# RWKV attention and GELU MLP on one core: orders behind the first MLP products searched at build, half of the negative powers made on ScalarE, the decays' transfer issued by ScalarE

## The chip, the cores and the metric

The kernel runs on one core of a Trainium2 chip. The metric is the device time of one execution in microseconds (us), as the median of several runs. Engines are named as in the profile: PE (TensorE matmul), PEld (TensorE weight load), DVE (VectorE), ACT (ScalarE), POOL (GpSimd) and SP (SyncE, which issues most transfers).

## The reference

A linear attention with decay per head and channel runs over 768 positions for 4 batches and 8 heads of 48 channels, and its output, 3072 tokens of 384 channels, goes through an MLP with 2048 hidden units.

```
for t in range(S):                       # S = 768, D = 48, f32
    cur = einsum('bhd,bhe->bhde', u * k[:, :, t], v[:, :, t])
    y[:, :, t] = einsum('bhd,bhde->bhe', r[:, :, t], state + cur)
    state = w[:, :, None] * state + einsum('bhd,bhe->bhde', k[:, :, t], v[:, :, t])
x = y.transpose(0, 2, 1, 3).reshape(3072, 384)
h = x @ w_in                             # 384 x 2048
g = 0.5 * h * (1 + erf(h / sqrt(2)))
out = g @ w_out                          # 2048 x 384
```

## The kernel before

**The MLP.** The tokens are cut into 6 chunks of 512 and the hidden units into 16 blocks of 128, which makes 96 steps; step m is block m mod 16 of chunk m div 16. Every f32 product is made of three with rounded operands: weights are split into a high part `wh` and a low part `wl`, activations into `xx` high and low. So a step has 9 products `Hp<-xx,wh/wl` into the one bank `Hp` (L696, step 1 alone goes into `O2`), two GELU activations on ACT (`gh`, the rounded result, L728, and `gf`, the full one, L729), a subtraction on DVE (`gl`, L730) and 9 products into the output banks `O` (L740). The next step's products into `Hp` have to wait until both activations have read it.

**The weights.** Block j's packed weights are loaded into one of three buffers, `raw[j % 3]` (L380, w_j below). ACT reads each buffer twice (`wa` L395, `wb` L398), DVE adds the two readings (L400), ACT rounds the sum to `wh` (L404) and DVE subtracts for `wl` (L407). A buffer can be loaded again once both readings are done. A load is one transfer on SP's queue.

**The attention.** 24 groups (`T`, `N`; later ones `Tb`, `Nb`), 4 to a chunk: the first four fill chunk 0 ahead of any MLP product, and the others stand as small products (L606 to L634) between the MLP steps. They use powers of the decays: `wu_sb` is loaded first on SP (L270), DVE makes the powers 1 to 64 by doubling and four RECIPROCALs of 64 columns make the negative ones (L333), ACT makes the next 64 powers for the states (L344, L346), and four transfers of SP copy both into `E` (L366). For the bonus term ACT or DVE multiply a diagonal by column sums `cs` into `Am` (L415), as the table `BONUS` says for each group and half.

**The order.** Nearly every operation is recorded with `add` or `dma` in `Plan` as engine, estimated duration, due time and dependences. `Plan.run` carries due times back along the dependences, and `Plan.play` simulates the engines: it always issues the operation that can start first, and of those that can start on an engine the one that is due first. The order in which `play` picks is the order on each engine. Until the first MLP product it also puts in products with no use (`HEATS`, L305).

Of the kernel before, what the change touches and what calls it, by code (L numbers as in the profile page):

```python
# [2 lines left out]

# [6 lines left out]
F32 = mybir.dt.float32  # L10
# [6 lines left out]
AF = mybir.ActivationFunctionType  # L17
# [6 lines left out]
C = 128  # L24
NCH = S // C
PAIRS = (3, 0, 1, 2)
NP = H // 2
NB = B
TOK = NB * C
NJ = DF // 128  # L30
HALF = 64
# [19 lines left out]

SCALE = ("dd", "d", "d", "d")
PRODUCT = ("d", "d", "d", "d")
BONUS = ("aa", "aa", "aa", "ad")


class Plan:
# [9 lines left out]
    DMA_QUEUED, DMA_SPREAD = 1200, 1050  # L67

    def __init__(self, after):
        self.after = after  # L70
        self.ops, self.writer, self.readers, self.reads, self.writes = [], {}, {}, [], []
        self.heats, self.heat_ns, self.heat_room, self.heat_from, self.heat_to = {}, 0, 0, None, None

    def add(self, eng, ns, at, fn, r=(), w=(), port=False):
        n = len(self.ops)
# [14 lines left out]
    def dma(self, nbytes, at, fn, r=(), w=()):  # L90
        self.add("sp", nbytes, at, fn, r, w)
# [7 lines left out]
        return self.OWN.get(e, 0) if self.ops[m][0] == e else self.LAG[e]  # L99

    def run(self):
        self.users = [[] for _ in self.ops]
        due = [o[2] for o in self.ops]
        for n in reversed(range(len(self.ops))):
# [5 lines left out]
    def play(self, due):  # L110

        ops = self.ops
        left = [len(o[4]) for o in ops]
# [4 lines left out]
        clear, unread, held, heating = {}, {}, None, False  # L118
        for n, k in enumerate(left):
            if not k:  # L120
                heapq.heappush(waiting[ops[n][0]], (0.0, n))
        for _ in ops:
            best, clash = None, float("inf")
            for e in self.LAG:
                wait, can = waiting[e], able[e]
                if not wait and not can:
                    continue
                start = max(free[e], lanes[0]) if e == "sp" else free[e]
                while wait and wait[0][0] <= start:
                    n = heapq.heappop(wait)[1]  # L130
# [12 lines left out]
                if best is None or start < best[0]:  # L143
                    best = (start, e, n)
            start, e, n = best
            while e == "pe" and heating:
                at = {b: max([free[e]] + [clear.get(x, 0.0) for x in b]) for b in self.heats
                      if not any(unread.get(x, 0) for x in b)}
                b = min(at, key=at.get, default=None)
                if b is None or at[b] + self.heat_room >= start:  # L150
                    break
                self.heats[b]()
# [6 lines left out]
            _, ns, _, fn, _, port = ops[n]  # L159
            if e == "sp":  # L160
                free[e] = start + self.DMA_GAP
                queued = bus - start - self.DMA_LEAD
                bus = max(bus, start + self.DMA_LEAD) + ns / self.DMA_RATES[start >= self.DMA_EARLY]
                end = bus + self.DMA_FIXED + self.DMA_SPREAD * (queued > self.DMA_QUEUED)
                lanes = lanes[1:] + [end]
            else:
                free[e] = end = start + ns
            ins = fn()
            if port:
                locked[e] = end  # L170
                if e == "dve":
                    held = ins
                elif held is not None:
                    self.after(ins, held, "port")
            if n in (self.heat_from, self.heat_to):
                heating = n == self.heat_from
            if heating:
                for b in [x for bank in self.heats for x in bank]:
                    if b in self.writes[n]:
                        unread[b] = unread.get(b, 0) + sum(b in self.reads[m] for m in self.users[n])  # L180
                    if b in self.reads[n]:
                        unread[b] = unread.get(b, 0) - 1
                        clear[b] = end + self.LAG[e]
            for m in self.users[n]:
                ready[m] = max(ready[m], end + self.lag(n, m))
                left[m] -= 1
                if not left[m]:
                    heapq.heappush(waiting[ops[m][0]], (ready[m], m))


def rwkv_gelu_mlp(tc, rkT, rkv, wuT, uN, wmlp, r, k, vT, w, u, out):
    nc = tc.nc
    with ExitStack() as ctx:
# [17 lines left out]
        wu_sb = sb([LP, 3 * NP], F32, "wu_sb", cst)  # L211
        w_sb = wu_sb[:, 0:NP]
# [10 lines left out]
        WKs = W[:, :, KEYS:]  # L223
# [112 lines left out]
        first = PAIRS[0]  # L336
        add("dve", 480, 6, lambda: inverse(first, first + 1), r=["P"], w=[f"W{first}"])
        for p in PAIRS[1:]:
            add("dve", 480, LATER, lambda p=p: inverse(p, p + 1), r=["P"], w=[f"W{p}"])


        def state_powers():
# [365 lines left out]
        def moe1(m, at):  # L708
# [8 lines left out]
            if m == 0:  # L717
                gaps0 = lambda k_: gaps[2 * k_:2 * k_ + 2]
                for k_ in range(3):
                    first = add("pe", 3 * MM, at + k_, lambda k_=k_: [  # L720
                        product1(x, j, n, (k_,), k_ == 0 and n == 0, k_ == 2 and n == 2) for n in range(3)],
                        r=["wh0", "wl0"] + xr("h", (k_,)) + xr("l", (k_,)) + gaps0(k_), w=["H"])
                    plan.heat_to = plan.heat_to or first
            else:
                for n in range(3):
                    add("pe", 3 * MM, at + n, lambda n=n: product1(x, j, n, start=n == 0, stop=n == 2, dst=dst),
                        r=[f"{('wh', 'wl', 'wh')[n]}{n1}"] + xr("hhl"[n]) + gaps, w=[H_])
# [15 lines left out]
        def moe2(m, at, dest):  # L743
# [27 lines left out]
            for i, (d, bank, a, b) in enumerate(parts):  # L771
# [11 lines left out]
            if not last:  # L783
# [224 lines left out]
```

## Time and profile before

| what | value |
|---|---|
| median of 3 runs | 478.93 us (478.65 to 478.95) |
| the profiled execution | 478.3 us, its span 476.6 us |
| granted TensorE clock | 1.00 of full speed |
| busy share of the span | PE 98%, DVE 48%, ACT 38%, POOL 14% |
| chain that ended last | PE 92%, DMA 4%, ACT 3% |
| moved by transfers | 46.60 MB |

The span is what the engines do from the first instruction to the last; the other 1.7 us lie around it. The chain that ended last is followed back from the last instruction, so its DMA and ACT shares tell what PE waited for before its unbroken stretch began.

### The profile page before, as it was taken

How to read it: one execution, taken by the hardware profiler on the slowest of the kernel's cores; microseconds unless marked ns; L12 is line 12 of the kernel's file. 1: busy time of each engine (PE TensorE's matmuls, PEld its weight loads, DVE VectorE, ACT ScalarE, POOL GpSimd, SP SyncE). 2: the span in 40 equal slices, each digit the busy share in tenths (PEclk: the TensorE clock that was granted, in tenths of full speed). 3: DMA queues.
4: the chain of work that ended last, by engine and by line, in shares of the span. 5: the costliest groups of instructions: out<-in, count | busy, mean ns of one | idle time of the engine just before them, and what ended most of it. 6: DMA issues, size and time to landing. Idle time of an engine off the chain costs nothing.

```text
span 476.6 us, 10284 instructions
## 1 busy us (share of the span) xinstructions
PE 469.2 (98%) x4525; PEld 378.3 (79%) x4525; DVE 230.7 (48%) x345; ACT 181.8 (38%) x333; POOL 67.6 (14%) x91
## 2 busy tenths in 40 slices
PE   8999999999999999999999999999999999999996
PEld 6767788888888787888888888888888887888875
DVE  7989989754354266153543543544435311211111
ACT  9998897233222223222223222223322222322221
POOL 1331021221020222010202202202112000000000
PEclk9999999999999999999999999999999999999999
DMA  8978682414023034031231330321402000100002
GB/s 306 362 296 312 231 265 91 122 48 155 25 83 106 2 114 153 1 106 39 69 106 67 96 99 9 106 54 52 162 15 91 14 0 12 66 1 1 1 0 72
DMA packets 15426, 46.60 MB, mean 98 GB/s; under 512 B 3664, under 2 KB 4048, under 8 KB 15376
## 3 DMA queue, kind: packets, MB, share of 16 engines
q1 hardware_dynamic: 15376, 45.88, 28.8%
q8 instruction: 37, 0.61, 0.5%
q14 instruction: 13, 0.11, 0.1%
HBM read 38.73 MB, written 4.72 MB: 91 GB/s over the span
## 4 chain that ended last, share of the span: by engine, by line
PE 92%; DMA 4%; ACT 3%; issue 0%; DVE 0%; ACTq 0%
PE Hp L696 42%; PE O L740 41%; PE Y L606 2%; DMA E<-W 2%; PE A L614 2%; PE Y L634 2%; PE A L623 1%; DMA raw<-in_wmlp_dram 1%; PE Y L740 1%; ACT W L344 0%; ACT Sa L530 0%; ACT wa L312 0%; ACT L291 0%; ACT wa L395 0%; ACT gh L728 0%; ACT gf L729 0%
## 5 line engine op out<-in xcount | busy, mean ns | idle before, releaser
L696 PE MATMUL Hp<-xx,wh 128*128 128x512 f32 x570 | 167.2, 401 | 0.0
L730 DVE TENSOR_TENSOR gl<-gf,gh 128x512 fp32r<-128x512 f32 x92 | 66.9, 727 | 166.4 <-ACT gf L729 166.1
L728 ACT ACTIVATE gh<-Hp 128x512 fp32r<-128x512 f32 x91 | 54.4, 598 | 213.9 <-PE Hp L696 213.8
L696 PEld LDWEIGHTS Hp<-xx,wh 128*128 128x128 f32 x570 | 104.4, 188 | 25.8 <-ACT gf L729 1.5
L696 PE MATMUL Hp<-xx,wl 128*128 128x512 f32 x285 | 82.1, 395 | 0.0
L740 PE MATMUL O<-gh,wh 128*128 128x512 f32 (+1 forms) x276 | 78.6, 391 | 0.5 <-ACT gf L729 0.5
L740 PE MATMUL O<-gh,wl 128*128 128x512 f32 (+1 forms) x276 | 78.6, 391 | 0.0
L740 PE MATMUL O<-gl,wh 128*128 128x512 f32 (+1 forms) x276 | 78.3, 390 | 0.0
L696 PEld LDWEIGHTS Hp<-xx,wl 128*128 128x128 f32 x285 | 53.6, 188 | 12.7
L740 PEld LDWEIGHTS O<-gh,wh 128*128 128x128 f32 x276 | 51.7, 188 | 13.5 <-ACT gf L729 0.9
L740 PEld LDWEIGHTS O<-gh,wl 128*128 128x128 f32 x276 | 51.2, 188 | 11.6
L740 PEld LDWEIGHTS O<-gl,wh 128*128 128x128 f32 x276 | 51.0, 188 | 11.4 <-issue 0.2
L729 ACT ACTIVATE gf<-Hp 128x512 f32<-128x512 f32 x95 | 56.3, 593 | 0.0
L561 POOL TENSOR_TENSOR Nb<-Nb 128x384 f32<-128x384 f32 x20 | 20.4, 1018 | 124.7 <-DMA Nb<-in_rkv_dram 75.4
L558 DVE TENSOR_TENSOR Tb<-Tb,E 112x1024 f32<-112x1024 f32 x20 | 25.4, 1268 | 2.3 <-DMA Tb<-in_rkT_dram 2.3
L663 DVE SCALAR_TENSOR_TENSOR Sb<-Sa,E,A 48x192 f32<-48x192 f32 x40 | 16.5, 413 | 18.1 <-PE A L623 17.5
L433 ACT CAST xx<-Y 112x512 fp32r<-112x512 f32 x15 | 8.8, 587 | 38.8 <-PE Y L634 38.7
L564 POOL TENSOR_TENSOR Nb<-Nb,WN 128x384 f32<-128x384 f32 x20 | 20.3, 1016 | 21.2 <-DVE wl L407 7.8
L567 POOL TENSOR_TENSOR Nb<-Nb,u_sb 128x384 f32<-128x384 f32 x20 | 20.3, 1013 | 17.8 <-DVE gl L730 12.5
L570 DVE TENSOR_REDUCE cs<-Nb 128x8 f32<-128x384 f32 x20 | 11.1, 553 | 18.1 <-POOL Nb L567 15.8
L644 POOL MEMSET done<- 1x1 f32 x19 | 1.7, 89 | 124.6 <-PE Y L606 124.6
L670 DVE COPY_PREDICATED Am<-past,A 128x512 f32<-128x512 uint32 x20 | 14.9, 747 | 7.0 <-PE A L623 6.8
(124 smaller groups left out, 388.9 us busy)
## 6 DMA issues: line engine op xcount, KB each, us to landing
raw<-in_wmlp_dram SPq DMA_DIRECT2D x16, 767.8 KB, 6.6
Nb<-in_rkv_dram SPq DMA_DIRECT2D x20, 576.0 KB, 5.6
Tb<-in_rkT_dram SPq DMA_DIRECT2D x20, 512.0 KB, 4.1
out_dram<-raw SPq DMA_DIRECT2D x5, 768.0 KB, 3.6
T<-in_rkT_dram SPq DMA_DIRECT2D x4, 512.0 KB, 5.0
xx<-x SPq DMA_DIRECT2D x30, 64.0 KB, 4.2
N<-in_rkv_dram SPq DMA_DIRECT2D x4, 384.0 KB, 7.0
out_dram<-raw SPq DMA_DIRECT2D x2, 256.0 KB, 2.1
```

What stands on the lines that cost most here:

```text
L558: add("dve", 1140, LATER, lambda: nc.vector.tensor_tensor(out=flat, in0=flat, in1=E[:, p, 0].rearrange("l h i -> l (h i)").unsqueeze(1).to ...
L561: add("pool", pool(DM), LATER, lambda: nc.gpsimd.tensor_tensor(out=n[:, 0], in0=n[:, 0], in1=n[:, 1], op=ALU.mult), r=[NK], w=[NR])
L564: add("pool", pool(DM), LATER, lambda: nc.gpsimd.tensor_tensor(out=kn, in0=kn, in1=WN2[:, p].rearrange("s j d -> s (j d)").unsqueeze(1).to ...
L567: add("pool", pool(DM), LATER, lambda: nc.gpsimd.tensor_tensor(out=n[:, 0], in0=n[:, 0], in1=u_sb[:, p, :].unsqueeze(1).to_broadcast([C, N ...
L570: add("dve", 465, LATER, lambda: nc.vector.tensor_reduce(out=sums, in_=n[:, 0].rearrange("s b (j d) -> s (b j) d", d=D), axis=AX.X, op=ALU ...
L663: add("dve", 430, at, lambda l=l, x=x: nc.vector.scalar_tensor_tensor(out=out[quarter(1 - x)], in0=src[l], scalar=E[l, p, 1, h, 32:33], in ...
L670: add("dve", 625, LATER, lambda: nc.vector.copy_predicated(out=am, mask=past2.bitcast(U32).unsqueeze(1).unsqueeze(1).to_broadcast([C, 2, N ...
L696: nc.tensor.matmul(dst, lhsT=wt[j][:, 0, k_ * 128:(k_ + 1) * 128], rhs=x[:, a, k_, :], start=start and k_ == ks[0], stop=stop and k_ == ks ...
L728: add("act", 480, LATER, lambda: nc.scalar.activation(out=high, in_=dst, func=AF.Gelu, scale=256.0), r=[H_], w=[GH])
L729: add("act", 480, LATER, lambda: nc.scalar.activation(out=gf, in_=dst, func=AF.Gelu, scale=256.0), r=[H_], w=["gf"])
L730: add("dve", dve(512), LATER, lambda: nc.vector.tensor_tensor(out=low, in0=gf, in1=high.bitcast(F32), op=ALU.subtract), r=["gf", GH], w=[G ...
L740: nc.tensor.matmul(dst[:, a:b], lhsT=wt[j][:, 1, d * 128:(d + 1) * 128], rhs=gt[:, a:b], start=(j == 0 and n == 0), stop=(j == NJ - 1 and ...
```

## The change

The edits are four. `wu_sb` is loaded by a transfer that ACT issues, as its first instruction, and no longer by SP. Each RECIPROCAL of 64 columns becomes one of 32 columns on DVE, and the other 32 columns are made by ACT as these times the 32nd negative power; the state powers are recorded behind them. The second half of the third group's bonus goes from ACT to DVE. The due times behind the first MLP product are changed at random 400 times while the kernel is built, each resulting order is replayed in `Plan`'s own model with four sets of durations, and the order that ends the last first-kind product of step 21 earliest in the model is issued. Further the output of the chunk before the last is written by three transfers in place of one, and there are 9 useless products in place of 10.

```diff
-HEATS, HEAT_NS, HEAT_ROOM, MM = 10, 300, 100, 233
+HEATS, HEAT_NS, HEAT_ROOM, MM = 9, 300, 100, 233
+SEARCH, REPLAYS, HEAT, SEED = 400, 4, 0.0, 2
-BONUS = ("aa", "aa", "aa", "ad")
+BONUS = ("aa", "aa", "ad", "ad")
...
     def run(self):
...
-        self.play(due)
+        chance = random.Random(SEED)
+        noise = [[1 + chance.gauss(0, 0.04) for _ in self.ops] for _ in range(REPLAYS)]
+        judged = lambda order: sum(self.replay(order, x) for x in noise)
+        order = self.play(due, self.judge)
+        end, near = judged(order), [
+            n for n in order[order.index(self.heat_to):] if isinstance(n, int) and self.ops[n][0] != "do"]
+        best, kept = end, due
+        for i in range(SEARCH):
+            other = list(due)
+            for n in chance.sample(near, chance.choice((1, 1, 2, 4))):
+                other[n] += chance.gauss(0, chance.choice((1500, 4000, 10000)))
+            got = judged(self.play(other, self.judge))
+            if got <= end + HEAT * REPLAYS * (1 - i / SEARCH) * chance.random():
+                end, due = got, other
+            if end < best:
+                best, kept = end, due
+        due = kept
+        self.issue(self.play(due))
...
-        dma(5000, -10 ** 6, lambda: nc.sync.dma_start(wu_sb, wuT), w=["w_sb"])
+        add("do", 1600, -10 ** 6, lambda: nc.scalar.dma_start(wu_sb, wuT), w=["w_sb"])
...
-        def inverse(p0, p1):
-            return nc.vector.reciprocal(out=W[:, p0:p1, 0:HALF], in_=W[:, p0:p1, C:HALF:-1])
+        def inverse(p, at):
+
+            add("dve", 300, at, lambda: nc.vector.reciprocal(
+                out=W[:, p, 32:HALF], in_=W[:, p, HALF + 32:HALF:-1]), r=["P"], w=[f"V{p}"])
+            add("act", 190, LATER, lambda: nc.scalar.activation(
+                out=W[:, p, 0:32], in_=W[:, p, 32:HALF], func=AF.Copy, scale=W[:, p, 32:33]), r=[f"V{p}"], w=[f"W{p}"])
...
-        add("act", 1700, LATER, state_powers, r=["P"], w=["WKs"])
+        add("act", 1700, LATER, state_powers, r=["P"] + [f"W{p}" for p in PAIRS], w=["WKs"])
...
+                if m == NJ + 5:
+                    plan.judge = last
...
+            if t == NCH - 2:
+                for d in range(3):
+                    dma(128 * 2048, at + 20000, lambda d=d: nc.sync.dma_start(
```

**ACT at the start.** `W` holds the powers, `diag` and `past` are masks, `wa` is a buffer being cleared, `cs` and `Am` belong to the first group's bonus. The rows stand behind the four that prepare `warm` and `spread`; L346 and L344 make the state powers. Before:

```order
L312 COPY wa_132<-zeros 128x768
L287 COPY diag_85<-diag 64x64
L312 COPY wa_133<-zeros 128x768
L346 COPY W<-W 112x4x32
L344 ACTIVATE W<-W 112x64 x4
L344 ACTIVATE W<-W 112x32 x4
L287 COPY diag_85<-diag 64x64
L287 COPY past_86<-past 64x64 x2
L475 COPY cs_117<-Hp 128x8
```

And after, where L402 is the new product, L414 and L412 the state powers:

```order
L378 COPY wa_133<-zeros 128x768
L402 ACTIVATE W<-W 112x32 x3
L353 COPY diag_85<-diag 64x64
L402 ACTIVATE W<-W 112x32
L353 COPY past_86<-past 64x64
L414 COPY W<-W 112x4x32
L412 ACTIVATE W<-W 112x64 x4
L412 ACTIVATE W<-W 112x32 x4
L543 COPY cs_117<-Hp 128x8
```

Ahead of the state powers there are now four products and two copies of masks, and ahead of everything the issue of a transfer.

**PE in the first two steps.** `wh_74` and `wl_78` are the weights of step 0, `wh_75` and `wl_79` those of step 1. Before:

```order
L525 MATMUL A<-N_110 48x48 x8
L696 MATMUL Hp<-xx_121,wh_74 128x512
L696 MATMUL Hp<-xx_121,wl_78 128x512
L696 MATMUL Hp<-xx_121,wh_74 128x512
L696 MATMUL O_72<-xx_121,wh_75 128x512 x3
L696 MATMUL O_72<-xx_121,wl_79 128x512 x3
```

And after:

```order
L593 MATMUL A<-N_110 48x48 x8
L764 MATMUL O_72<-xx_121,wh_75 128x512 x3
L764 MATMUL Hp<-xx_121,wh_74 128x512
L764 MATMUL Hp<-xx_121,wl_78 128x512
L764 MATMUL Hp<-xx_121,wh_74 128x512
L764 MATMUL O_72<-xx_121,wl_79 128x512 x3
```

Three products of step 1 moved ahead of the last three of step 0, so that the latter stand between the use of `wh_75` and that of `wl_79`.

**ACT around step 5.** `wa` and `wb` read the weights of `raw` (raw1 is w7, raw2 w8, raw0 behind that w9), `wh6` is a rounding, `gh` and `gf` are the GELUs. Before, from the second reading of w7 to the GELU of step 5 (`gh1`, the last but two here):

```order
L395 ACTIVATE wa1_133<-raw1_130 128x768
L728 ACTIVATE gh0_124<-Hp_69 128x512
L729 ACTIVATE gf_128<-Hp_69 128x512
L398 ACTIVATE wb2_136<-raw2_131 128x768
L404 CAST wh6_438<-wb0_134 128x768
L395 ACTIVATE wa0_132<-raw2_131 128x768
L728 ACTIVATE gh1_125<-Hp_69 128x512
L729 ACTIVATE gf_128<-Hp_69 128x512
L398 ACTIVATE wb0_134<-raw0_129 128x768
```

And after, from the GELU of step 3 (`gf`, the first row) to that of step 5:

```order
L799 ACTIVATE gf_128<-Hp_69 128x512
L466 ACTIVATE wb1_135<-raw1_130 128x768
L463 ACTIVATE wa1_133<-raw1_130 128x768
L463 ACTIVATE wa0_132<-raw0_129 128x768
L798 ACTIVATE gh0_124<-Hp_69 128x512
L799 ACTIVATE gf_128<-Hp_69 128x512
L472 CAST wh6_443<-wb0_134 128x768
L463 ACTIVATE wa0_132<-raw2_131 128x768
L466 ACTIVATE wb2_136<-raw2_131 128x768
L466 ACTIVATE wb0_134<-raw0_129 128x768
L798 ACTIVATE gh1_125<-Hp_69 128x512
L799 ACTIVATE gf_128<-Hp_69 128x512
```

The first reading of w9, `wb0<-raw0`, moved from behind the GELU of step 5 to ahead of it. Both readings of w7 and the second of w6 stand behind the GELU of step 3, and they free the buffers of w10 and w9.

**SP around the same place.** The weight transfers from w6 on, whose buffers are raw0, raw1 and raw2 in turn (w6, w7, w8, w9, w10), and those of a later group, `Tb0` and `Nb0`. Before:

```order
L380 DMA raw0_129<-in_wmlp_dram 128x3071
L380 DMA raw1_130<-in_wmlp_dram 128x3071
L380 DMA raw2_131<-in_wmlp_dram 128x3071
L264 DMA Tb0_97<-in_rkT_dram 128x1024
L268 DMA Nb0_111<-in_rkv_dram 128x1152
L380 DMA raw0_129<-in_wmlp_dram 128x3071
L380 DMA raw1_130<-in_wmlp_dram 128x3071
```

And after:

```order
L448 DMA raw0_129<-in_wmlp_dram 128x3071
L448 DMA raw1_130<-in_wmlp_dram 128x3071
L334 DMA Nb0_111<-in_rkv_dram 128x1152
L330 DMA Tb0_97<-in_rkT_dram 128x1024
L448 DMA raw2_131<-in_wmlp_dram 128x3071
L448 DMA raw1_130<-in_wmlp_dram 128x3071
L448 DMA raw0_129<-in_wmlp_dram 128x3071
```

The group's transfers moved ahead of w8, and w10 is now issued ahead of w9, so that w9 stands behind `Nb0`, `Tb0`, w8 and w10.

## Rows read from the trace of the kernel before

**Rows 1.** Windows: busy time of the engines, granted clock, DMA share, GB/s.

```profile
5.00:24.00 19.00, 18.39 (x214) 14.45 (x214) 18.20 (x23) 18.06 (x54) 3.96 (x4) 1.00 1.05 382
...
34.00:62.00 28.00, 28.00 (x283) 21.81 (x285) 27.00 (x36) 25.22 (x36) 5.48 (x7) 1.00 0.72 245
...
43.00:52.00 9.00, 9.00 (x38) 6.73 (x37) 8.91 (x13) 8.53 (x13) 1.02 (x1) 1.00 0.89 315
...
60.00:400.00 340.00, 339.89 (x3597) 274.20 (x3596) 162.43 (x248) 106.50 (x188) 54.80 (x71) 1.00 0.25 79
```

**Rows 2.** Chain that ended last, 0 to 60 us: start, us, what.

```profile
4.89 1.82 ACT W L344 x8
...
7.69 10.84 DMA E<-W
...
18.54 6.31 DMA raw<-in_wmlp_dram
...
39.16 0.59 PE Y L606 x32
...
41.03 2.30 PE Hp L696 x9
43.33 1.65 PE O L740 x6
...
47.08 1.40 PE O L740 x6
48.48 2.30 PE Hp L696 x9
```

**Rows 3.** Timeline of SP's queue from 0 us: start, duration, operation.

```profile
0.81 0.41 SPq L270 DMA_DIRECT2D wu_sb<-in_wuT_dram  x1
1.28 1.36 SPq L264 DMA_DIRECT2D T<-in_rkT_dram  x3
```

**Rows 4.** Timeline of ACT, 4 to 8 us.

```profile
4.79 1.91 ACT L344 ACTIVATE W<-W 112x64 f32<-112x64 f32 x8
...
6.98 0.50 ACT L287 COPY past<-past 64x64 f32<-64x64 f32 x2
```

**Rows 5.** Timeline of DVE, 5 to 11 us.

```profile
5.08 0.69 DVE L465 TENSOR_TENSOR RK<-T 112x512 f32<-112x512 f32 x1 [0.45 <-DMA T<-in_rkT_dram]
5.69 1.37 DVE L333 RECIPROCAL W<-W 112x64 f32<-112x64 f32 x3
...
10.24 1.30 DVE L489 COPY_PREDICATED Am<-past,A 128x1024 f32<-128x1024 uint32 x1 [0.30 <-ACT Am L415]
```

**Rows 6.** Timeline of PE, 23 to 32 us.

```profile
23.64 0.50 PE L696 MATMUL Hp<-xx,wh 128*128 128x512 f32 x1
...
26.89 0.86 PE L696 MATMUL O<-xx,wh 128*128 128x512 f32 x3
27.90 0.96 PE L696 MATMUL O<-xx,wl 128*128 128x512 f32 x3
...
31.42 0.50 PE L740 MATMUL O<-gh,wh 128*128 128x512 f32 x1 [0.47 <-ACT gf L729]
```

**Rows 7.** Timeline of ACT, 33 to 52 us.

```profile
33.70 1.10 ACT L395 ACTIVATE wa<-raw 128x768 f16<-128x768 bf16 x1
34.65 0.89 ACT L398 ACTIVATE wb<-raw 128x768 int32<-128x768 uint32 x1
...
50.82 0.60 ACT L728 ACTIVATE gh<-Hp 128x512 fp32r<-128x512 f32 x1
51.31 0.59 ACT L729 ACTIVATE gf<-Hp 128x512 f32<-128x512 f32 x1
```

**Rows 8.** Weight transfers, issue to landing: all 16 (median), at 43.5, at 55.9 us.

```profile
raw<-in_wmlp_dram SPq DMA_DIRECT2D x16, 767.8 KB, 6.6
...
raw<-in_wmlp_dram SPq DMA_DIRECT2D x1, 767.8 KB, 7.5
...
raw<-in_wmlp_dram SPq DMA_DIRECT2D x1, 767.8 KB, 4.2
```

More of the change, by code (lines that the diff above doesn't have):

```diff
@@ L1 @@
 import heapq
+import random
 from contextlib import ExitStack
@@ L66 @@
     DMA_EARLY, DMA_RATES = 5000, (400.0, 345.0)
-    DMA_QUEUED, DMA_SPREAD = 1200, 1050
+    DMA_QUEUED, DMA_SPREAD, DMA_UNEVEN = 1200, 1050, 550
     def __init__(self, after):
@@ L72, in __init__ @@
         self.heats, self.heat_ns, self.heat_room, self.heat_from, self.heat_to = {}, 0, 0, None, None
+        self.judge = None
     def add(self, eng, ns, at, fn, r=(), w=(), port=False):
@@ L101, in run @@
     def run(self):
+        count = len(self.ops)
         self.users = [[] for _ in self.ops]
         due = [o[2] for o in self.ops]
-        for n in reversed(range(len(self.ops))):
+        for n in reversed(range(count)):
             for d in self.ops[n][4]:
@@ new lines, in run, with land, replay @@
+        self.issue(self.play(due))
+    def land(self, start, bus, ns, slow=1.0):
+        queued = bus - start - self.DMA_LEAD
+        bus = max(bus, start + self.DMA_LEAD) + ns * slow / self.DMA_RATES[start >= self.DMA_EARLY]
+        return bus + self.DMA_FIXED + self.DMA_SPREAD * (queued > self.DMA_QUEUED), bus
+    def replay(self, order, slow):
+        ops, ends = self.ops, {}
+        free = {e: 800.0 for e in self.LAG}
+        bus, locked, lanes = 0.0, {"dve": 0.0, "pool": 0.0}, [0.0] * self.DMA_LANES
+        for n in order:
+            if not isinstance(n, int):
+                free["pe"] += self.heat_ns
+                continue
+            e, ns, _, _, deps, port = ops[n]
+            start = free[e]
+            for d in deps:
+                start = max(start, ends[d] + self.lag(d, n))
+            if port:
+                start = max(start, locked["pool" if e == "dve" else "dve"])
+            if e == "sp":
+                start = max(start, lanes[0])
+                free[e] = start + self.DMA_GAP
+                ends[n], bus = self.land(start, bus, ns, slow[n])
+                lanes = lanes[1:] + [ends[n]]
+            else:
+                free[e] = ends[n] = start + ns * (slow[n] if e != "pe" else 1.0)
+            if port:
+                locked[e] = ends[n]
+        return ends[n]
@@ L112, in play, with issue @@
+    def issue(self, order):
+        held = None
+        for n in order:
+            if not isinstance(n, int):
+                self.heats[n]()
+                continue
+            ins = self.ops[n][3]()
+            if self.ops[n][5]:
+                if self.ops[n][0] == "dve":
+                    held = ins
+                elif held is not None:
+                    self.after(ins, held, "port")
+    def play(self, due, stop=None):
         ops = self.ops
+        order = []
         left = [len(o[4]) for o in ops]
@@ L117, in play @@
         bus, locked, lanes = 0.0, {"dve": 0.0, "pool": 0.0}, [0.0] * self.DMA_LANES
-        clear, unread, held, heating = {}, {}, None, False
+        clear, unread, heating = {}, {}, False
         for n, k in enumerate(left):
@@ L151, in play @@
                     break
-                self.heats[b]()
+                order.append(b)
                 free[e] = at[b] + self.heat_ns
@@ L158, in play @@
                 heapq.heapify(waiting[e])
-            _, ns, _, fn, _, port = ops[n]
+            _, ns, _, _, _, port = ops[n]
+            order.append(n)
             if e == "sp":
                 free[e] = start + self.DMA_GAP
-                queued = bus - start - self.DMA_LEAD
-                bus = max(bus, start + self.DMA_LEAD) + ns / self.DMA_RATES[start >= self.DMA_EARLY]
-                end = bus + self.DMA_FIXED + self.DMA_SPREAD * (queued > self.DMA_QUEUED)
+                end, bus = self.land(start, bus, ns)
                 lanes = lanes[1:] + [end]
@@ L167, in play @@
                 free[e] = end = start + ns
-            ins = fn()
             if port:
                 locked[e] = end
[L171 to L174, printed above, removed]
             if n in (self.heat_from, self.heat_to):
@@ L188, in play @@
                     heapq.heappush(waiting[ops[m][0]], (ready[m], m))
+            if n == stop:
+                break
+        return order
 def rwkv_gelu_mlp(tc, rkT, rkv, wuT, uN, wmlp, r, k, vT, w, u, out):
@@ L330, in powers @@
             return last
-        def inverse(p0, p1):
-            return nc.vector.reciprocal(out=W[:, p0:p1, 0:HALF], in_=W[:, p0:p1, C:HALF:-1])
+        def inverse(p, at):
[3 more added lines that the diff above has]
+                out=W[:, p, 0:32], in_=W[:, p, 32:HALF], func=AF.Copy, scale=W[:, p, 32:33]), r=[f"V{p}"], w=[f"W{p}"])
         add("dve", 1500, 5, powers, r=["w_sb"], w=["P"], port=True)
[L336 to L339, printed above, removed]
+        for n, p in enumerate(PAIRS):
+            inverse(p, LATER if n else 6)
         def state_powers():
@@ L725, in moe1 @@
                 for n in range(3):
-                    add("pe", 3 * MM, at + n, lambda n=n: product1(x, j, n, start=n == 0, stop=n == 2, dst=dst),
+                    last = add("pe", 3 * MM, at + n, lambda n=n: product1(x, j, n, start=n == 0, stop=n == 2, dst=dst),
                         r=[f"{('wh', 'wl', 'wh')[n]}{n1}"] + xr("hhl"[n]) + gaps, w=[H_])
+                if m == NJ + 5:
+                    plan.judge = last
             add("act", 480, LATER, lambda: nc.scalar.activation(out=high, in_=dst, func=AF.Gelu, scale=256.0), r=[H_], w=[GH])
@@ L782, in moe2 @@
                     dma(512 * (b - a), at + 2000, lambda d=d, a=a, b=b, o=o: nc.sync.dma_start(dest[d][:, a:b], o), r=[R])
-            if not last:
+            if t == NCH - 2:
+                for d in range(3):
+                    dma(128 * 2048, at + 20000, lambda d=d: nc.sync.dma_start(
+                        dest[d], flat2(raw[0]).bitcast(F32)[:, d * TOK:(d + 1) * TOK]), w=[f"raw0{d}"])
+            elif not last:
                 dma(128 * 6144, at + 20000, lambda: nc.sync.dma_start(
```

1 line of the change is left out of this document (removed).

## The prediction

> **What bounds the kernel now.** I read the windows first. From 34 us on PE is busy without a gap: 28.00 of 28 us, 9.00 of 9, and later 339.89 of 340 at a granted clock of 1.00 [rows 1]. An edit that takes work from ACT, DVE or SP there gains nothing by itself. What counts is how much of PE's work is done when its unbroken stretch begins, and whether a new wait is put into it. So next I followed the chain of waits from the start, where PE does not yet appear: ACT's state powers, the transfers into `E` (10.84 us from 7.69), then the third weight's transfer, which lands at 18.54 + 6.31 = 24.85 [rows 2]. Between 5 and 24 us the transfers move 382 GB/s at a DMA share of 1.05, so they are what the start is made of [rows 1].
>
> PE's first MLP product starts at 23.64 [rows 6]. From there I count three waits. Three products take 1.40 / 2 = 0.70 us, since six take 1.40 [rows 2]; those of step 1 start at 26.89 and the next three at 27.90, so 1.01 - 0.70 = 0.31 us goes to waiting for `wl` [rows 6]. At 31.42 PE has waited 0.47 for `gf` [rows 6]. And in the chain a piece of six products takes 1.65 from 43.33 where another takes 1.40, a wait of 0.25 behind step 3 [rows 2]. Together that is 1.03 us. The steps from 60 us on hold no loss that the change could take out.
>
> **The transfer on ACT.** SP's first two issues start at 0.81 and 1.28 [rows 3], so without the first all later transfers may be issued 0.47 earlier. DVE waits 0.45 us for `T` at 5.08 [rows 5], and between 5 and 24 us the queue is full [rows 1], so the shift may pass to all that lands later. It is not free: ACT, which stands on the chain at that place [rows 2], must issue the transfer first. No row has an issue by ACT; I bound it by nothing below and by SP's 0.47 above, and take 0.47, the only issue of that transfer there is.
>
> **The split reciprocals.** Three RECIPROCALs take 1.37 us, 0.46 each [rows 5]. No row has 32 columns; bounds are 0.23 (half) and 0.46 (no saving). DVE thus saves 0 to 0.9 us over four, and I take the half. ACT gains four products. Eight scalings of 64 and 32 columns take 1.91, 0.24 each [rows 4], so four cost up to 0.96; I take 0.90, as they are all short. The order puts a mask of `diag` and one of `past`, 0.50 together [rows 4], ahead of the state powers too. So the fourth state power, which `E` needs, moves from 4.79 + 4 x 0.24 = 5.75 to 5.75 + 0.47 + 0.90 + 0.50 = 7.62. The transfers into `E` start at 7.69 now [rows 2]: ACT uses up all the slack they had, and `E` starts no earlier. What is queued ahead of it still lands up to 0.47 earlier, and the queue is full, so I let the third weight land 0.1 to 0.47 earlier and take 0.3: 24.55. Behind the powers on ACT stands the first group's bonus, about 1.1 us later than now; DVE already waits 0.30 us for it at 10.24 [rows 5]. DVE has products of later groups to move ahead, so I cost this at nothing; without that cover it is up to 1.1 us of DVE time ahead of the first MLP product. The third bonus's move to DVE is work of the same stretch and is taken with it.
>
> **The order behind the first products.** `wh` of step 1 comes out of ACT behind the first reading of the third weight. Counted with ACT's durations and one activation cast that now stands between, it is there at about 26.9, no earlier than its use at 26.89 [rows 6]. PE now asks for it 0.70 earlier, as the last three products of step 0 stand behind it, and waits; these three then hide the 0.31 us of `wl`. The 0.47 us wait for `gf` is covered by products of step 2 and the group that moved ahead of it. Counting products to the same amount of work, PE is 0 to 0.4 us ahead when the unbroken stretch begins: **-0.15**, nearer to nothing, since `wh` is not earlier.
>
> The wait behind step 3 goes, because six second products fewer stand ahead of that step and are there to fill it: **-0.25**. In its place step 3's nine products stand in one piece, and `wl` follows `wh` by 0.31 more than three products [rows 6]: 0 to 0.3, **+0.15**.
>
> **Step 5 and the ninth weight, w9.** Before, step 3's first products end at 41.03 + 2.30 = 43.33 [rows 2], with 24 second products done; after, with 18. So they end at 43.33 - 6 x 0.233 - 0.15, about 41.8. The GELU pair takes 0.49 + 0.59 = 1.08 us [rows 7], to 42.9. Then ACT reads w7 twice and w6 once, 0.89 to 1.10 each and 0.95 from one start to the next [rows 7]: w10 is issued at about 44.7 and w9 at 45.6. Step 5's products end at 48.48 + 2.30 = 50.78 now [rows 2]; after, nine more second products stand ahead, so 50.78 + 2.10 - 0.25 = 52.63. Behind them PE has a group's small products, 41.03 - 39.16 = 1.87 us [rows 2], and then wants `Hp` free at 54.5. ACT must have read it, and ahead of that stands the first reading of w9: 54.5 less 1.08 of GELU, 0.89 of reading and the hand-over means that w9 has to be there by about 52.5. How long does it take? Its neighbours decide: 4.2 us for a transfer alone, 6.6 as the median, and 7.5 for the one that had a weight and a group ahead of it [rows 8]. That makes 49.8, 52.2 or 53.1, and a wait of 0 to 0.6. With a weight and part of a group ahead the last row is nearest; I take the middle, **+0.3**.
>
> By the Trainium skill, "DMA: Bandwidth & Descriptors", sections Specifications and Anatomy of one DMA, a core's HBM limit is about 358 GB/s and a transfer's fixed part about 2.0 us; that makes about 4.2 us for a weight, as an estimate, w9 in time and a sum lower by 0.3. The lone transfer agrees at 4.2 us; the one with neighbours, 7.5 us, does not [rows 8].
>
> **The sum.** -0.15 - 0.25 + 0.15 + 0.3 = +0.05. Against the profiled execution's 478.3 that is 478.35. The median of the runs shown, 478.93, is 0.63 above that execution, and the sum carries over: 479.0. The last chunks' output in three transfers comes while PE still has a whole chunk to do, and costs nothing. By the terms' bounds this case reaches from 478.3 to 479.8.
>
> **Rivals.**
> - *w9 holds up ACT (slower).* When step 3 ends at 41.8 and ACT turns to w7, two transfers of a group (0.59 and 0.52 MB) and three weights (0.79 each) have to land, 3.47 MB. At the 315 GB/s of 43 to 52 us that is 11.0 us, to 52.8; at the 245 GB/s of 34 to 62 us it is 14.2 us, to 56.0 [rows 1]. The wait is then 0.3 to 3.5 us, the GELU of step 5 stands behind it on ACT, and PE behind that: 479.0 to 482.2, a middle of 480.6. It decides once w9 lands after 53.7. Against it: the lower rate includes stretches in which nothing was asked for. Chance 0.27.
> - *The start passes in full (faster).* All three waits go (1.03 us) and the 0.47 us of SP reaches PE, -1.5: 477.4; it is measurably faster from -0.96 on. For it: DVE waits for `T` and the queue is full. Against it: `E` waits for ACT, and `wh` of step 1 is bound by its order on ACT. Chance 0.23.
> - *ACT delays the start (no change).* If the products or the issue take more than I allow, `E` starts later, by some 0.3 us, and the gain of 0.15 turns round: 479.4. Chance 0.10.
> - My forecast has the remaining 0.40.
>
> **How the numbers follow.** 0.2%, 0.96 us, is about what a measurement of this kernel can tell from no change. The forecast and the third rival lie within it and make 0.50 for the same; the others make 0.23 for faster and 0.27 for slower. The likeliest time is 479.0. The range takes in most of the faster rival, from 477.8, and the lower half of the slower one, to 480.6. It leaves out some 0.2 in all.
>
> **What would show it.** In the profile after, `T` should be issued at 0.8, `E` at about 7.7, and the third weight should land at about 24.55; if `E` starts earlier, ACT's term is too large. PE's first product should stand within 0.5 us of 23.64. Step 1 should wait for `wh` near 26.9. Behind step 3 there should be no wait of 0.25. Near 54.5 the chain shows whether PE waited for a GELU, ACT ahead of it for `raw`, and when w9 landed. The prediction is wrong if w9's landing costs more than a microsecond, if the start comes more than 0.7 us earlier or later, or if a wait shows after 60 us, where I expect none.

## The result and the profile after

The changed kernel takes 484.37 us (median of 19 runs, 480.07 to 486.52) against 479.23 us before (19 runs): a ratio of 1.0086, 95% interval 1.006 to 1.0112. The forecast of 479.0 and its range to 480.6 were wrong; it is slower. The runs fall into two groups, seven from 480.07 to 482.49 and twelve from 484.18 to 486.52; one of the 19 runs of the kernel before, 484.54, is as long too, and what that one lost is not on record. The profiled execution is one of the first, 480.14 us with a span of 478.4, 1.8 us over that of before. So two things are to be found: these 1.8 us, and what the twelve runs lose besides.

The chain that ended last, at the start (start, duration, what):

```profile
0.81 3.99 DMA wu_sb<-in_wuT_dram
4.81 0.02 issue
4.83 0.18 DVE W L388
```

The transfer of the decays stands at its head. Among the transfers' issues (size, time from issue to landing) of the kernel after it reads

```profile
T<-in_rkT_dram SPq DMA_DIRECT2D x1, 512.0 KB, 3.8
wu_sb<-in_wuT_dram ACTq DMA_DIRECT2D x1, 5.2 KB, 4.0
```

and the same transfer in the kernel before

```profile
wu_sb<-in_wuT_dram SPq DMA_DIRECT2D x1, 5.2 KB, 1.6
```

Issued at 0.81 in both, it lands 2.4 us later. DVE's timeline after shows who waits (start, duration, operation, idle time before and who ended it):

```profile
4.83 0.17 DVE L388 TENSOR_SCALAR W<-wu_sb 112x4 f32<-112x4 f32 x1 [3.31 <-DMA wu_sb<-in_wuT_dram]
5.04 1.40 DVE L393 TENSOR_TENSOR W<-W 112x4 f32<-112x4 f32 x6
6.36 0.98 DVE L400 RECIPROCAL W<-W 112x32 f32<-112x32 f32 x4
7.25 0.63 DVE L533 TENSOR_TENSOR RK<-T 112x512 f32<-112x512 f32 x1
```

RK comes at 7.25, not at 5.08 [rows 5]: with the powers late, T is no longer what it waits for. ACT and SP's queue follow, with the new products, the state powers and the transfers into `E`, which start at 9.41, not 7.69 [rows 2, 4]:

```profile
6.74 0.74 ACT L402 ACTIVATE W<-W 112x32 f32<-112x32 f32 x3 [1.60 <-DVE W L400]
...
8.32 1.91 ACT L412 ACTIVATE W<-W 112x64 f32<-112x64 f32 x8
```

```profile
0.81 1.34 SPq L330 DMA_DIRECT2D T<-in_rkT_dram  x3
...
9.41 3.84 SPq L434 DMA_DIRECT2D E<-W  x4
```

And PE, which did not wait here before (the first row is its last two useless products):

```profile
5.57 1.05 PE L371 MATMUL Hp<-zeros 128*128 128x512 f32 x2
7.94 1.13 PE L538 MATMUL Hp<-wu_sb,RK 112*128 112x96 f32 x8 [1.32 <-DVE RK L533]
...
25.53 0.50 PE L764 MATMUL Hp<-xx,wh 128*128 128x512 f32 x1
...
27.98 0.96 PE L764 MATMUL O<-xx,wh 128*128 128x512 f32 x3
```

The first MLP product starts at 25.53, 1.89 us later than the 23.64 of before [rows 6], and the span ends 1.8 us later. Between them nothing is gained or lost on balance; from 60 to 400 us PE is as full as before [rows 1].

```profile
60.00:400.00 340.00, 339.76 (x3475) 273.05 (x3474) 160.12 (x248) 107.90 (x189) 53.93 (x68) 1.00 0.25 78
```

### The profile page after: what moved, and what is told of

Its sections match the earlier page's. It is cut to its first block, busy times and chain, and to the rows that moved or that the text cites. A ratio compares the mean times of both kernels' runs of the same rounds, so it can differ in the third digit from the quotient of the medians.

```text
span 478.4 us, 10308 instructions
## 1 busy us (share of the span) xinstructions
PE 470.4 (98%) x4526; PEld 378.6 (79%) x4526; DVE 227.8 (48%) x346; ACT 180.8 (38%) x333; POOL 69.5 (15%) x91
## 4 chain that ended last, share of the span: by engine, by line
PE 87%; DVE 6%; ACT 4%; DMA 2%; issue 1%; ACTq 0%
PE Hp L764 39%; PE O L810 37%; PE Y L674 2%; PE Y L702 2%; PE A L682 2%; DMA raw<-in_wmlp_dram 1%; PE A L691 1%; PE Y L810 1%; DVE wl L475 1%; DVE gl L800 1%; DMA wu_sb<-in_wuT_dram 1%; PE O L571 1%; DVE wb L468 1%; ACT gh L798 1%; ACT wh L472 1%
## 5 line engine op out<-in xcount | busy, mean ns | idle before, releaser
L764 PE MATMUL Hp<-xx,wh 128*128 128x512 f32 x570 | 167.2, 401 | 0.2
L800 DVE TENSOR_TENSOR gl<-gf,gh 128x512 fp32r<-128x512 f32 x92 | 65.0, 707 | 170.1 <-ACT gf L799 165.9
```

The source lines that it names most:

```text
L764: nc.tensor.matmul(dst, lhsT=wt[j][:, 0, k_ * 128:(k_ + 1) * 128], rhs=x[:, a, k_, :], start=start and k_ == ks[0], stop=stop and k_ == ks ...
```

## The experiments

The theory after the result: the transfer lands late when ACT issues it at the moment at which SP issues its first T, and in most runs a lower pace of PE follows its wait for the powers. The rivals: the four products on ACT and the new orders make the start late; and what the twelve runs lose lies at step 5 or is spread over the steps.

**act_transfer_alone.** Only who issues the transfer, in the kernel before; all orders stay.

```diff
-        dma(5000, -10 ** 6, lambda: nc.sync.dma_start(wu_sb, wuT), w=["w_sb"])
+        dma(5000, -10 ** 6, lambda: nc.scalar.dma_start(wu_sb, wuT), w=["w_sb"])
```

> The kernel before with the decays' transfer issued by ACT and nothing else changed, the order of all other instructions as before. Theory (the transfer lands late when ACT issues it beside SP's first T): it lands about 4.0 us after its issue at 0.81, as in the changed kernel, where it took 1.6 before; DVE's powers start near 4.8, PE's first MLP product near 25.5, and the time is 480 to 481, with single runs of 484 to 486. Rival (the later start of the changed kernel comes from the four products on ACT and the new order): the transfer lands by 2.5, the first product stays within 0.5 us of 23.64, and the time is 478.4 to 479.2.

Measured: 484.17 us (483.27 to 487.71, 6 runs), ratio 1.0106 (1.0083 to 1.0128). This one line alone loses 4.9 us by the medians, where the whole change loses 5.1; all six runs are long, and none lies at the 480 to 481 that I expected. The transfer took 3.8 us. The profiled execution is the longest, 487.71 us, and its first MLP product starts at 33.38, far behind the 25.5 expected. PE's timeline shows why:

```profile
4.71 1.05 PE L305 MATMUL A<-zeros 128*128 128x512 f32 x2
5.57 0.63 PE L305 MATMUL Y<-zeros 128*128 128x512 f32 x1
7.43 2.03 PE L470 MATMUL Hp<-wu_sb,RK 112*128 112x96 f32 x8 [1.24 <-DVE RK L465]
...
12.60 2.02 PE L470 MATMUL Hp<-wu_sb,RK 112*128 112x96 f32 x8
...
27.60 1.16 PE L484 MATMUL Y<-Ts 64*128 64x128 f32 x16
...
33.38 0.50 PE L696 MATMUL Hp<-xx,wh 128*128 128x512 f32 x1
```

From its wait of 1.24 us until 27.60 every product takes nearly twice its time, called half pace below; the same eight products took 1.13 us in the kernel after. The wait did not bring the half pace about here: the useless products ahead of it ran at it already (1.05 us for two, where two such products take 0.63 at full pace), as they do at the start of every profiled execution. What is missing is the rise to full pace, which the kernel before had near 5.9 us.

**sp_transfer_back.** The changed kernel with SP issuing the transfer first.

```diff
-        add("do", 1600, -10 ** 6, lambda: nc.scalar.dma_start(wu_sb, wuT), w=["w_sb"])
+        nc.sync.dma_start(wu_sb, wuT); add("do", 1600, -10 ** 6, lambda: None, w=["w_sb"])
```

> The changed kernel with the decays' transfer issued by SP as its first, as before; the order of all other instructions as in the changed kernel. Theory (late landing): it lands 1.6 us after its issue, the powers start near 2.4, the first MLP product stands near 23.6 to 24.0, the time is 478.0 to 479.0 and no run is above 481. Rival (products and order): the time stays at 480 or above, with runs of 484 to 486.

Measured: 479.86 us (479.15 to 481.36, 11 runs), ratio 1.0012 (1.0002 to 1.0022). The transfer lands after 1.7 us, the first MLP product starts at 24.34, and no run is above 481.4, so the theory holds in the main; but the time is 0.9 above the upper end that I gave. What remains of the change costs 0.6 us, by this interval 0.1 to 1.1. Its start is the one that I had in fact forecast, and its profile answers the forecast's steps below.

**both_transfers.** SP also issues a copy of the decays, into a tile of its own that nothing reads.

```diff
-        w_sb = wu_sb[:, 0:NP]
+        wu_too = sb([LP, 3 * NP], F32, "wu_too", cst); w_sb = wu_sb[:, 0:NP]
...
-        add("do", 1600, -10 ** 6, lambda: nc.scalar.dma_start(wu_sb, wuT), w=["w_sb"])
+        nc.sync.dma_start(wu_too, wuT); add("do", 1600, -10 ** 6, lambda: nc.scalar.dma_start(wu_sb, wuT), w=["w_sb"])
```

> The changed kernel, in which SP also issues a copy of the decays, that nothing reads, ahead of its first T; ACT's transfer is still the one that is read, and both are issued at about 0.8. T is issued 0.47 later again. If ACT's transfer lands late because T's 512 KB start beside it, it now lands near 2.4 to 2.8 as SP's copy does, and the time is 478.5 to 479.5. If a transfer that ACT issues lands late by itself, SP's copy lands after 1.6 us, ACT's still after about 4.0, and the time is 480.5 to 481 or above.

Measured: 476.22 us (475.47 to 476.92, 4 runs), ratio 0.994 (0.9922 to 0.9957). The landing speaks for T's transfers: with T issued at 1.29 and a small transfer ahead of it, ACT's lands 1.9 us after its issue. The time is 2.3 below what either theory allowed. PE's busy time says where it comes from, the first row of the page, against 469.2 before:

```profile
PE 463.7 (98%) x4526; PEld 378.4 (80%) x4526; DVE 229.9 (49%) x346; ACT 180.5 (38%) x333; POOL 71.5 (15%) x91
```

As many products take 5.5 us less. The extra tile moves what lies behind it; the next kernels take the two effects apart.

**after_again.** The changed kernel once more.

> The changed kernel as it is, for a second profile. Its runs on record reach from 480.07 to 486.52, and the profiled one is among the lowest. Theory: the runs of 484 to 486 lose another 4 to 6 us where PE waits at the start, near 6.6 to 8 us, and a lower granted clock follows the wait in part of them. Rival: they lose it in a wait at step 5 for the ninth weight, or in waits spread over the steps. A profile of such a run shows the place; one near 480 tells nothing on it.

Measured: 484.66 us (480.07 to 485.98, 12 runs), ratio 1.0081 (1.0055 to 1.0108). The profiled execution is the one of 485.98. PE's timeline, and two windows with the granted clock (the third number from the end):

```profile
4.72 0.66 PE L371 MATMUL A<-zeros 128*128 128x512 f32 x2
5.21 0.63 PE L371 MATMUL Hp<-zeros 128*128 128x512 f32 x2
7.75 1.64 PE L538 MATMUL Hp<-wu_sb,RK 112*128 112x96 f32 x8 [1.91 <-DVE RK L533]
...
11.33 2.02 PE L538 MATMUL Hp<-wu_sb,RK 112*128 112x96 f32 x8
...
21.79 1.14 PE L538 MATMUL Hp<-wu_sb,RK 112*128 112x96 f32 x8
...
30.79 0.50 PE L764 MATMUL Hp<-xx,wh 128*128 128x512 f32 x1
```

```profile
7.75:21.79 14.04, 14.04 (x92) 12.48 (x92) 10.19 (x12) 10.08 (x36) 1.95 (x2) 0.52 1.06 384
21.79:30.00 8.21, 8.21 (x107) 6.36 (x107) 6.16 (x8) 7.27 (x16) 3.14 (x4) 1.00 0.78 275
```

Here PE is at full pace before its wait (0.66 and 0.63 us for two products). It waits 1.91 us, then is busy throughout for 14.04 us at a clock of 0.52, that is about 1.2 GHz, and returns to 2.4 GHz. Its first MLP product starts 5.26 us later than in the other profiled execution, and the span, 484.2, is 5.8 us longer. So the loss of this long run lies at the start but for 0.40 us, which PE waits at 61.49 for the GELU of step 5; ACT had waited 2.60 us for w9 ahead of it. Seven of the 12 runs are long.

**copy_same_tiles.** SP's unread copy goes into a weight buffer that is filled later, so that no tile moves.

```diff
-        add("do", 1600, -10 ** 6, lambda: nc.scalar.dma_start(wu_sb, wuT), w=["w_sb"])
+        nc.sync.dma_start(raw[2].rearrange("p a b c -> p (a b c)").bitcast(F32)[0:LP, 0:3 * NP], wuT); add("do", 1600, -10 ** 6, lambda: nc.scalar.dma_start(wu_sb, wuT), w=["w_sb"])
```

> As the kernel with both transfers, but SP's unread copy of the decays goes into a weight buffer that is loaded later, so that no tile is added or moves. Theory (T's transfers beside it make ACT's transfer land late): ACT's transfer lands within 2.2 us of its issue as it did there (1.9), PE's first MLP product starts between 24.3 and 25.0, no run is above 481.5, and with PE's matmuls at the pace of the changed kernel the time is 479.5 to 480.3; the 476.2 us there then come from the added tile. Rival (the copy itself saves the time): 476 to 477.

Measured: 480.44 us (479.30 to 482.04, 8 runs), ratio 1.0028 (1.0012 to 1.0044). The issues:

```profile
T<-in_rkT_dram SPq DMA_DIRECT2D x1, 512.0 KB, 3.9
raw<-in_wuT_dram SPq DMA_DIRECT2D x1, 5.2 KB, 1.7
wu_sb<-in_wuT_dram ACTq DMA_DIRECT2D x1, 5.2 KB, 1.9
```

Both small transfers land early, the first MLP product starts at 24.49, and no run is above 482.1. The copy gives back most of the late start, and no run is long; the median lies 0.1 above the range that I gave, and two runs 0.4 and 0.5 above the bound. A transfer that ACT issues is thus not slow by itself. Whether T's delay of 0.47 us or the small transfer ahead of T on SP's queue does it is not separated.

**three_more_idle_products.** The changed kernel with three more products of no use at PE's start.

```diff
-            for n in range(HEATS):
+            for n in range(HEATS + 3):
```

> The changed kernel with three more of the useless products at its start, 1.3 us of PE work, the order otherwise as in the changed kernel. Theory (PE's wait for RK near 6.6 to 8 us is what the lower clock follows): the wait before the first useful product falls from 1.3 to 1.9 us to below 0.6, the products behind it run at full pace in nearly all runs, the runs lie between 480 and 481, none at 484 to 486, and the transfer's 2 us at the start remain. Rival (the lower pace has to do with something else, as the late powers): most runs stay at 484 to 486.

Measured: 481.03 us (480.38 to 482.24, 6 runs), ratio 1.004 (1.0027 to 1.0052). PE still waits, but less, and no run is long:

```profile
7.93 1.13 PE L538 MATMUL Hp<-wu_sb,RK 112*128 112x96 f32 x8 [0.82 <-DVE RK L533]
```

The transfer takes 4.0 us as in the changed kernel. None of these 6 runs is long, and 19 of the changed kernel's 31 are: the half pace of the long runs hangs on the stretch that the useless products fill. The edit shortens PE's wait and also gives PE more work ahead of it, and which of the two counts is not separated. This kernel takes 2.0 us more than the kernel before, sp_transfer_back 0.6 us more; the difference is about that of their starts, 25.51 and 24.34. The wait fell less than I had expected, since the last of the added products already ran at full pace and took less time.

**wide_decays_before** and **wide_decays_after_sp.** The decays' tile takes 96 bytes in place of 48, in the kernel before and in the changed one with SP's transfer; tiles behind it move up by 32 bytes, as the build allots them.

```diff
-        wu_sb = sb([LP, 3 * NP], F32, "wu_sb", cst)
+        wu_sb = sb([LP, 6 * NP], F32, "wu_sb", cst)[:, 0:3 * NP]
```

> The kernel before, with the decays' tile 96 bytes wide in place of 48, of which it uses the first 48; all later tiles of that pool move by 48 bytes, the order stays. Theory (the faster matmuls of the kernel with both transfers come from where the tiles lie): PE's busy time falls from 469.2 by 4 to 6 us and the time to 473.5 to 475.5. Rival (they come from something else in that kernel): 478.5 to 479.5.

> The changed kernel with the decays' transfer issued by SP, and with the decays' tile 96 bytes wide. Theory (placement, and the rest of the change worth nothing): 474 to 476, 0.3 to 1.0 above the kernel before with the wide tile. Rival (placement has no part): 479.5 to 480.2, as with the transfer on SP alone.

Measured: 481.11 us (480.26 to 482.07, 5 runs), ratio 1.0044 (1.0031 to 1.0057), and 482.78 us (481.47 to 484.61, 6 runs), ratio 1.0074 (1.0055 to 1.0093). Both miss, in the other direction: PE's busy time stays (469.9 and 470.4), and PE waits for `E`, 1.38 and 2.26 us, where the kernels without the wide tile waited not at all and 0.76. The expectation spoke of 48 bytes; the build moved the tiles by 32, and in both_transfers by 64.

**spare_tile_before** and **spare_tile_after_sp.** An unused tile of 64 bytes behind the decays, so that the tiles lie as in both_transfers.

```diff
-        wu_sb = sb([LP, 3 * NP], F32, "wu_sb", cst)
+        wu_sb = sb([LP, 3 * NP], F32, "wu_sb", cst); spare = sb([LP, 16], F32, "spare", cst)
```

> The kernel before with an unused tile of 64 bytes behind the decays' tile, so that all later tiles of the lower half, xx, gh, gl, E, raw and the first four wh and wl among them, lie 64 bytes higher, where they lay in the kernel with both transfers; with the wide tile they lay 32 bytes higher. The order stays. Theory (PE's pace depends on where these tiles lie, and E's transfers on the 64 bytes): PE's busy time falls from 469.2 to 463 to 465, PE's wait for E is below 0.5 us, and the time is 473.5 to 475.5. Rival (the pace came from something else in that kernel): 478.5 to 479.5.

> The changed kernel with the decays' transfer issued by SP, with the same unused tile of 64 bytes. Theory: 474 to 476, and 0.3 to 1.0 above the kernel before with the unused tile, as the two are apart without it (479.86 and 479.26): what is left of the change is worth nothing or a little less. Rival (the new orders pay once the start is in place): at least 0.5 below it.

Measured: 475.10 us (474.73 to 476.27, 4 runs), ratio 0.9909 (0.9895 to 0.9924), and 475.83 us (474.39 to 478.06, 6 runs), ratio 0.9938 (0.9915 to 0.996). The place gives the pace, though PE's busy time in spare_tile_before is 465.6, just above the range that I gave: behind its wait for `E` this execution ran 3.24 us at half pace, at a clock of 0.50.

```profile
21.42 0.98 PE L354 MATMUL O<-ident,E 112*128 112x112 f32 x4 [1.63 <-DMA E<-W]
```

```profile
21.42:24.66 3.24, 3.24 (x21) 2.43 (x21) 1.81 (x2) 0.54 (x1) 1.61 (x2) 0.50 1.06 328
```

The part on `E` fell: PE waits for it 1.6 and 1.2 us. Between the two kernels the difference is 0.7 us, with intervals that overlap.

**orders_unsearched.** The changed kernel with SP's transfer and with no search.

```diff
-SEARCH, REPLAYS, HEAT, SEED = 400, 4, 0.0, 2
+SEARCH, REPLAYS, HEAT, SEED = 0, 4, 0.0, 2
```

> The changed kernel with the decays' transfer issued by SP and with no search, so that the orders are those of the plain due times; the split reciprocals, the bonus and the three output transfers stay. With the search it took 479.86. If the search is worth what its model says, it is slower, 480.2 or more. If the split reciprocals cost the 0.6 us and the search is worth nothing, 479.6 to 480.1. If the searched orders cost it, 479.0 to 479.4.

Measured: 480.60 us (479.85 to 482.60, 11 runs), ratio 1.0035 (1.0022 to 1.0048), against 1.0012 (1.0002 to 1.0022) with the search. By the medians the search is worth about 0.7 us, with intervals that touch, and what is left of the change without it costs about 1.3 us. That is the split reciprocals, the bonus, the three output transfers, one useless product less and the orders that follow from them; which of these does it is not separated.

**spare_tile_at_xx.** The unused tile ahead of `xx` in the kernel before.

```diff
-        xx = [sb([128, 2, 3, TOK], F32R, f"xx{i}") for i in range(2)]
+        spare = sb([128, 16], F32, "spare"); xx = [sb([128, 2, 3, TOK], F32R, f"xx{i}") for i in range(2)]
```

> The kernel before with the unused tile of 64 bytes placed ahead of xx: xx, x3, gh, gl, raw, wa and wb lie 64 bytes higher, E, Tb, Nb, Am and all wh and wl where they lay before. Theory (what PE streams, xx, gh and gl, sets its pace by where it lies, and E's transfers got slower by E's place): PE's busy time is 463 to 465, PE waits less than 0.5 us for E, the time is 473 to 475.5. Rival (the four wh and wl that had moved set it): PE's busy time stays at 469 and the time at 478.5 to 479.5.

Measured: 471.24 us (470.74 to 471.86, 5 runs), ratio 0.9833 (0.9819 to 0.9846): faster than both kernels, and below the range that I gave. The page, part 1 and a row of the costliest groups, which read 469.2, and 167.2 and 401 ns, before:

```profile
PE 461.3 (98%) x4525; PEld 377.9 (80%) x4525; DVE 230.4 (49%) x345; ACT 181.6 (39%) x333; POOL 67.6 (14%) x91
...
L696 PE MATMUL Hp<-xx,wh 128*128 128x512 f32 x570 | 164.3, 396 | 0.0
```

The weights did not move, so it is not they that set the pace. PE waits 0.91 us for `E`, which did not move either, so E's place does not explain that wait.

## Why the prediction was wrong

**The step that failed is "The transfer on ACT".** It asked what the issue costs ACT and what leaving SP's first slot gives, 0.47 us each, and let the landing stand at what it was. But SP's first slot had been more than an issue: a small transfer stood in it ahead of T's 512 KB. Without it the transfer takes 4.0 us in place of 1.6, the powers start at 4.83 in place of 2.43, and the first MLP product starts 1.89 us later. T's own row [rows 3] moved to 0.81 as forecast, and what I had counted as a gain came with the loss. The issue itself had been priced right, at 0.47: ACT's first operation behind it starts at 1.26 in place of 0.81.

Not all of the 1.89 us is the transfer's. With SP issuing it again, in sp_transfer_back, the first MLP product starts at 24.34: 1.19 us hang on the transfer, and 0.70 on the products and orders (below). Between these two kernels the powers are 2.26 us apart and the product only 1.19. Most of this difference is in two waits that sp_transfer_back has and the changed kernel does not: DVE's for T, 0.20 us, and PE's for `E`, 0.76.

The Trainium skill, "DMA: Bandwidth & Descriptors", section Issuing engines are not separate DMA queues, says that transfers of all engines run on the same 16 DMA engines and interleave, and that issuing on several engines only saves the issuing time. The trace agrees with the saving: T is issued 0.47 us earlier. That the small transfer lands at about the time that T does, 4.8 and 4.6 us, fits the shared engines.

**The second loss was in no case of the prediction.** With RK at 7.25, PE runs out of useless products near 6.6 us in the kernel after, and in three profiled executions with the late transfer it waits 1.2 to 1.9 us. Behind this wait PE ran at half pace for 14 and 20 us in two of the three, and the start comes 5 to 8 us later. Twelve of the 19 runs are about as long as such an execution; that they lost it the same way is inferred from these two profiles. I had read PE's waits from 23.64 on, and none of those ahead of it, since the chain of before does not touch PE there [rows 2]. What stood between PE and a wait was only the row of useless products, and no term asked what happens when a later RK uncovers it.

**The other terms, in sp_transfer_back.** There the start is in place, and the terms can be read:

```profile
6.18 1.91 ACT L412 ACTIVATE W<-W 112x64 f32<-112x64 f32 x8
```

```profile
19.72 0.58 PE L422 MATMUL O<-ident,E 112*128 112x112 f32 x4 [0.76 <-DMA E<-W]
...
24.34 0.50 PE L764 MATMUL Hp<-xx,wh 128*128 128x512 f32 x1
...
27.55 0.97 PE L764 MATMUL O<-xx,wh 128*128 128x512 f32 x3 [0.70 <-ACT wh L472]
...
55.28 0.96 PE L764 MATMUL Hp<-xx,wh 128*128 128x512 f32 x3 [0.29 <-ACT gf L799]
```

- The split: four RECIPROCALs of 32 columns take 0.98 us, 0.25 each, so the half that I took was right. The state powers begin at 6.18 in place of 4.79, that is 1.39 later, for 1.40 forecast without the issue. E's transfers start at 8.13, where I had said about 7.7, and PE waits 0.76 for them.
- The start: taken as 0.15 to the good, it is 0.70 to the bad at the first MLP product, 24.34 for 23.64, and still 0.62 where the unbroken stretch begins, as the next wait (0.70) stands for two of before (0.31 and 0.47). This is the second step that failed. The third rival, that ACT delays the start, had the direction and half the size.
- `wh` of step 1: PE waits 0.70 for it, at the place forecast.
- Step 3: the wait of 0.25 is gone, as forecast, and no wait for `wl` took its place; the 0.15 was not needed. The step's nine products do not stand in one piece, as I had read: three second products lie between `wh` and `wl`, at 40.35.
- w9: I had it issued at 45.6 and landing at 52.2 to 53.1, with a wait of 0 to 0.6. It is issued at about 46.7 and takes 6.6 us. ACT waits 1.90 us for it, until 53.29, with the GELU of step 5 behind it, and PE then waits 0.29:

```profile
53.29 0.97 ACT L466 ACTIVATE wb<-raw 128x768 int32<-128x768 uint32 x1 [1.90 <-DMA raw<-in_wmlp_dram]
54.14 0.60 ACT L798 ACTIVATE gh<-Hp 128x512 fp32r<-128x512 f32 x1
```

The 0.29 for my 0.3 is luck. In the changed kernel, with the late start, PE does not wait there at all: step 6 follows its group at 55.63. In other executions with the same orders it waits 0.40 (after_again), 0.55 (spare_tile_after_sp), 0.79 (copy_same_tiles), 1.13 (both_transfers) and 1.35 us (three_more_idle_products). The last of them, first PE, then ACT:

```profile
57.02 0.97 PE L764 MATMUL Hp<-xx,wh 128*128 128x512 f32 x3 [1.35 <-ACT gf L799]
```

```profile
55.09 0.91 ACT L466 ACTIVATE wb<-raw 128x768 int32<-128x768 uint32 x1 [3.00 <-DMA raw<-in_wmlp_dram]
```

So the slower rival, w9, is real and its cost differs from execution to execution. In four of these kernels w9 lands at 54.1 to 55.1, behind the 53.7 from which I had let it decide; over six of the executions it took 5.9 to 7.8 us from its issue, and never the 4.2 of the estimate in the prediction. It is not what made the changed kernel slower: the profiled execution has none of it, and the long one 0.40 us.

With the transfer at its place the change measures +0.6 us (0.1 to 1.1) where I had +0.05. In this execution the steps behind the start came out near their prices; the start, 0.77 from its price, did not. One wait of 0.15 us for a GELU stands at 72.49, past the 60 us behind which I expected none.

## What to carry to other kernels

The first slot of a queue is not only an issue's cost: whoever leaves it lets the next large transfer start earlier, beside the small one that everything waits for (4.0 us in place of 1.6 here). Before moving a transfer, read its time from issue to landing, and ask what will be issued at the same moment then; the edit by itself, as one kernel, shows it in one run. And where a stretch of filler work covers a wait of PE, count what it costs when it ends too early: here, in the long runs, about 5 us for a wait of less than 2 us.

## What the runs showed of the hardware

- **A small transfer beside a large one.** 5.2 KB took 1.6 to 1.8 us from SP's first slot, 1.9 us from ACT with a small transfer ahead of T on SP's queue, and 3.8 to 4.0 us from ACT with T issued at the same moment.
- **PE's pace after a wait.** Of eight waits of 1.2 to 2.3 us behind PE's first product in the profiled executions, three stood ahead of half pace: 1.91 (after_again), 1.63 (spare_tile_before) and 1.24 us (act_transfer_alone). Behind 1.32 (the kernel after), 1.38 (wide_decays_before), 2.26 (wide_decays_after_sp), 1.24 (spare_tile_after_sp) and 1.35 us (three_more_idle_products, near 57) PE ran at full pace. So the length of the wait alone does not decide. Nor does the pace before it: in after_again and spare_tile_before it was full, in act_transfer_alone and the kernel after half. What decides is open. In after_again and spare_tile_before the clock row shows 0.52 and 0.50. In act_transfer_alone, and for the first useless products of every execution, the same doubled durations stand under a clock of 1.00, so there the durations tell what the row does not:

```profile
7.43:27.60 20.17, 20.17 (x120) 17.06 (x120) 12.85 (x17) 13.28 (x43) 0.61 (x1) 1.00 0.97 348
```

- **Where tiles lie.** With `xx`, `x3`, `gh`, `gl`, `gf`, `raw`, `wa` and `wb` 64 bytes higher, PE's busy time falls from 469.2 to 461.3 us with the same products, three of which take 0.84 in place of 0.86 us in the steady stretch. With those and all other tiles of that half 64 bytes higher it is 465.6, half pace included (spare_tile_before), and 463.7 in the changed kernel with SP's transfer (spare_tile_after_sp, 469.2 without the tile); with all 32 bytes higher it is 469.9. Which tile does it, and why, is open; of the tiles that moved PE reads only `xx`, `x3`, `gh` and `gl`.
- **PE's wait for `E`** differs between kernels of one order from nothing to 1.6 us (the kernel before and its versions with moved tiles), and in none of them does it follow E's place alone. This too is open.
